# Float64 weights converted in place, with four load buffers and whole pieces per slot, in an attention and mixer kernel

## The chip, the cores and the metric

The kernel runs on one core of one Trainium2 chip. A core has TensorE (PE) for matrix products, VectorE (DVE), ScalarE (ACT) and GpSimd (POOL) for elementwise work, and SyncE (SP), which here only issues transfers. Each takes its own instructions in the order in which the program hands them over. The metric is the device time of the whole kernel in microseconds (us), the median of several runs.

## The reference

Thresholded attention over 8 batches and 8 heads of 576 tokens with 64 columns, then a mixer of two small networks over 512 columns:

```python
scores = scale * np.matmul(q, k.transpose(0, 1, 3, 2))
thresh = np.max(scores, axis=-1, keepdims=True) - tau
scores = np.where(scores >= thresh, scores, -1000000000.0)
attn = np.exp(scores - np.max(scores, axis=-1, keepdims=True))
attn = attn / (np.sum(attn, axis=-1, keepdims=True) + 1e-09)
x = heads side by side of np.matmul(attn, v)          # (8, 576, 512)
h = np.maximum(x.transpose(0, 2, 1) @ w_tok1, 0.0) @ w_tok2
u = x + h.transpose(0, 2, 1)
out = u + np.maximum(u @ w_ch1, 0.0) @ w_ch2
```

The four weight matrices (576x256, 256x576, 512x1536, 1536x512) are scaled by a numpy float64 number when they are made, and so arrive as float64. [...] the kernel makes the float32 values itself, from the two 32-bit halves of each number.

## The kernel before

**Units.** The main loop runs over 144 units (b, w, t), 18 for each of the 8 batches. A unit u covers one block of 128 query rows of two heads. In the order of the code it does the following:

- `scores(u)`: PE makes the scores (L286), DVE takes their maximum (L291, two instructions), POOL turns the maxima into a bias (L292).
- `norm(u - 1)`: DVE takes the reciprocal of the row sums (L310, L311), POOL scales the weights e with it (L314, two instructions).
- The turn of unit u - 2. In batch 0 PE transposes e in three groups (L337), and DVE, or now and then ACT, copies each to eT (L339). In later batches `turn_blocks` transposes on DVE into T (L348), and SP moves the blocks with 16 transfers (L358) whenever a group is complete.
- `weigh(u)`: ACT makes e from the scores, with two Prelu (L301) and two Exp (L304).
- `values`, when due: PE multiplies eT by the values (pv, L388 and L393), ACT copies the result to xT (L398).
- In later batches, mixer steps from the queue `todo`, in up to three places of a unit, by `fill`. `push` fills the queue once a batch has all its values, for batch 0 in unit 20. Its steps are `turn_x` (L412, copied by L413), `tok1` (L422, relu L423), `tok2` (L429, added to xT by DVE at L433), `ch1` (L451, relu L452) and `ch2` (L467).
- `load_qk`, `load_v` and, in some units, `prep`, which transposes q and k of a coming pair on DVE (L268).

A score buffer comes free only when `weigh` has read it, and the two buffers of the mixer's products when ACT or DVE has read them.

**Weights.** The matrices are cut into 31 pieces: two of w1 with 512 columns and one of 64 rows by 256, four of w2 with 288 columns, then 12 of wc1 and 12 of wc2 with 512. `load_piece` brings a piece from HBM into one of three parts of a scratch tile (the tile later serves as xT); SP issues it (L196). `f64_to_f32` converts it with six instructions: on ACT a Copy (L159) of the low words, written over them, and a Square (L160) of the high words into the one buffer h2; on DVE a shift (L161), a sign operation (L164) and a mask (L167), which reads h2; on POOL an add (L168) of the low part, which writes the weight. Between shift and add the value lies in one of two buffers a. Both functions are Python generators: they issue a part and then yield, so that a piece takes three steps.

- Step 1: Copy, Square, shift. Step 2: sign. Step 3: mask, add, and the load of the piece three further on.
- `weight(n)` takes n steps. It stands in two places of a unit: ahead of `weigh(u)`, and after the values. In batch 0 each place takes one step, later four and three.
- `need(i)` takes steps until piece i is converted; the mixer's steps call it ahead of their first use of a weight.

`tc.manual_schedule()` keeps the instructions of every engine in the order in which this code issues them.

Of the kernel before, what the change touches and what calls it, by code (L numbers as in the profile page):

```python
# [9 lines left out]
F32 = mybir.dt.float32  # L10
U32 = mybir.dt.uint32
I32 = mybir.dt.int32
I64 = mybir.dt.int64
AF = mybir.ActivationFunctionType
ALU = mybir.AluOpType
# [6 lines left out]
def kernel(  # L22
# [26 lines left out]
    nc = tc.nc  # L49
# [81 lines left out]

    WMAX = 512
    scratch = work.tile([P, NP * 2 * S], U32, tag="xT", name="scratch")
    NRAW = 3
    raw_at = [scratch[:, 2 * WMAX * i : 2 * WMAX * (i + 1)] for i in range(NRAW)]
    a_at = [scratch[:, 2 * WMAX * NRAW + WMAX * i : 2 * WMAX * NRAW + WMAX * (i + 1)] for i in range(2)]
    sq_at = scratch[:, 2 * WMAX * NRAW + 2 * WMAX : 2 * WMAX * NRAW + 3 * WMAX].bitcast(F32)
    turn_of = [0]

    def like(x, dst):  # L140
        if len(dst.shape) == 2:
            return x
        return x.rearrange("p (a b) -> p a b", a=dst.shape[1])

    def f64_to_f32(dst, raw, rows, n):

        lo, hi = raw[:, :, 0], raw[:, :, 1]
        a = a_at[turn_of[0] % 2][0:rows, 0:n]
        h2 = sq_at[0:rows, 0:n]
        turn_of[0] += 1
        af = a.bitcast(F32)
        nc.scalar.activation(out=lo.bitcast(I32), in_=lo, func=AF.Copy, scale=2.0**-29)  # L159
        nc.scalar.activation(out=h2, in_=hi.bitcast(F32), func=AF.Square)  # L160
        yield nc.vector.tensor_scalar(  # L161
            out=a, in0=hi, scalar1=3, scalar2=0x3FFFFFFF, op0=ALU.logical_shift_left, op1=ALU.bitwise_and
        )
        yield nc.vector.scalar_tensor_tensor(  # L164
            out=a, in0=hi, scalar=0xC0000000, in1=a, op0=ALU.bitwise_and, op1=ALU.bitwise_or
        )
        nc.vector.scalar_tensor_tensor(out=af, in0=h2, scalar=2.0**-30, in1=af, op0=ALU.is_ge, op1=ALU.mult)  # L167
        nc.gpsimd.tensor_tensor(  # L168
            out=dst.bitcast(I32), in0=like(a.bitcast(I32), dst), in1=like(lo.bitcast(I32), dst), op=ALU.add
        )  # L170

    pieces = [
        (w1[:, 2 * i : 2 * i + 2, :], moe_w_tok1[2 * P * i : 2 * P * i + 2 * P, :].rearrange("(t p) x -> p t x", p=P))
        for i in range(NI // 2)
    ]
# [9 lines left out]
    raws = {}  # L185

    def load_piece(i):
        dst, src = pieces[i]
        rows = dst.shape[0]
        n = 1  # L190
        for d in dst.shape[1:]:
            n *= d
        wide = src.dtype == I64
        raw = raw_at[i % NRAW][0:rows, 0 : n * (2 if wide else 1)]
        raw = raw.bitcast(src.dtype)
        nc.sync.dma_start(out=like(raw, dst), in_=src)  # L196
        raws[i] = raw, rows, n

    def weight_ops():
        for i, (dst, src) in enumerate(pieces):  # L200
            raw, rows, n = raws.pop(i)
            if src.dtype == I64:
                for _ in f64_to_f32(dst, raw.bitcast(U32).rearrange("p (n w) -> p n w", w=2), rows, n):
                    yield
            else:
                yield
                yield
                nc.gpsimd.tensor_copy(out=dst, in_=like(raw, dst))
            if i + NRAW < len(pieces):
                load_piece(i + NRAW)  # L210
            yield

    wops = weight_ops()
    steps_done = 0

    def weight(n):

        nonlocal steps_done
        for _ in range(n):
            if next(wops, wops) is wops:  # L220
                return
            steps_done += 1

    def need(i):

        weight(3 * i + 3 - steps_done)

    load_piece(0)
    load_qk(1, (nc.sync, nc.sync))
# [30 lines left out]
    def in_blocks(b):  # L260
        return b > 0
# [10 lines left out]
    def scores(u):  # L272
        b, p0, t = units[u]
        sc = [
            (ps_3rd if b == 0 and (2 * u + h) % 3 == 2 else ps_sc).tile([P, 2, MAIN], F32, tag="sc", name=f"sc{h}_{u}") for h in range(2)
        ]
        if t == SHARED:
            parts = [(b * NP + p0 + i, slice(MAIN, S), slice(64 * i, 64 * i + 64)) for i in range(2)]
        else:
            i, c = divmod(t - (t > SHARED), NI)  # L280
            parts = [(b * NP + p0 + i, slice(P * c, P * c + P), slice(0, P))]
        order = [(f, part, h) for f in range(2) for part in parts for h in range(2)]
        for f, (n, cols, rows), h in order if b else sorted(order, key=lambda o: o[2]):
            r = slice(D * h, D * h + D)
            qT, kT = heads[n]
            nc.tensor.matmul(sc[h][rows, f, 0:HS], lhsT=qT[r, cols], rhs=kT[r, HS * f : HS * f + HS], start=True, stop=True)  # L286
        mx = small.tile([P, 2], F32, tag="mx", name=f"mx_{u}")
        bias = small.tile([P, 2], F32, tag="bias", name=f"bias_{u}")
        for h in range(2):
            c = slice(h, h + 1)  # L290
            nc.vector.tensor_reduce(out=mx[:, c], in_=sc[h][:, :, 0:HS], axis=AX.XY, op=ALU.max)  # L291
            nc.gpsimd.tensor_scalar(out=bias[:, c], in0=mx[:, c], scalar1=toff, scalar2=-SCALE, op0=ALU.add, op1=ALU.mult)  # L292
        st[u] = sc, bias
# [13 lines left out]
    def norm(u):  # L307
        e, rs = st[u]
        rr = small.tile([P, 2], F32, tag="rr", name=f"rr_{u}")
        nc.vector.tensor_scalar(out=rr, in0=rs, scalar1=1e-9, scalar2=None, op0=ALU.add)  # L310
        nc.vector.reciprocal(out=rr, in_=rr)  # L311
        for h in range(2):
            eh = e[:, S * h : S * h + S]
            nc.gpsimd.tensor_scalar(out=eh, in0=eh, scalar1=rr[:, h : h + 1], scalar2=1.0, op0=ALU.mult, op1=ALU.mult)  # L314
        st[u] = e

    def group_of(u):

        b, p0, t = units[u]
        if t == SHARED:  # L320
            return (b, p0, "s"), 0, 1
        i, c = divmod(t - (t > SHARED), NI)
        return (b, p0 + i, c // 2), c % 2, 2
# [38 lines left out]
    def split_middle(n):  # L362

        lv, vl = vals[n], vlast[n % VL]
        for h in range(2):
            r = slice(D * h, D * h + D)
            nc.gpsimd.tensor_copy(out=vl[r, r], in_=lv[r, NI, :])
        vals[n] = lv, vl
# [142 lines left out]
    b_now = 0  # L511
    LAG = 2
    for u in range(len(units) + LAG + 4):
        on = u < len(units)
        if u == UB:
            late.close()
            ps_mm = ctx.enter_context(tc.tile_pool(name="ps_mm", bufs=2, space=bass.MemoryType.PSUM))
        if on:
            b_now, p0, t = units[u]
            n = b_now * NP + p0  # L520
        w = u - LAG
        back = 0 <= w < len(units)
        if on:
            scores(u)
        if 0 < u <= len(units):
            norm(u - 1)
        if back:
            key, place, many = group_of(w)
            if in_blocks(key[0]):
                turn_blocks(w)  # L530
            else:
                for i in range(3):
                    turn(w, i)
            if place == many - 1:
                b, p, c = key
                if c == 0 and p % 2 == 0:
                    split_middle(b * NP + p)
                if c == "s":
                    split_middle(b * NP + p + 1)
                when = u + (2 if in_blocks(b) else 1)  # L540
                due += [(when, b, p + i, c) for i in range(2 if c == "s" else 1)]
        if b_now:
            fill(0.4)
        weight(4 if b_now else 1)
        if on:
            weigh(u)
        if b_now:
            fill(0.3)
        while due and due[0][0] <= u:
            _, b, p, c = due.popleft()  # L550
            values(b, p, c)
            if p == NP - 1 and c == 1:
                push(b)
        if b_now:
            fill(0.3)
        weight(3 if b_now else 1)
        if on:
            m = n + 2 + t // 4
            if t < 8 and m < len(pairs):
                load_qk(m, (nc.scalar if b_now else nc.sync,) * 2, t % 4)  # L560
                if t % 4 == 3:
                    load_v(m)
            if t == 2:
                prep(n + 1)
            if t == 7 and n + 2 < len(pairs):
                prep(n + 2)
    weight(10000)
    quota = 1e9
    fill(1.0)
# [28 lines left out]
```

## Time and profile before

| what | value |
|---|---|
| median of 3 runs | 1424.96 us (1424.34 to 1425.93) |
| the profiled execution: its time, its span | 1424.03 us, 1421.9 us |
| PE busy, share of the span | 1346.7 us, 95% |
| DVE, ACT, POOL busy | 584.1, 589.8, 345.4 us |
| mean granted PE clock | 0.984 |
| Copy L159, Square L160, median of 31 | 0.676, 0.659 us |
| shift L161, sign L164, mask L167, median of 31 | 0.421, 0.823, 0.692 us |
| add L168 with 512 columns, median | 1.367 us |
| first Copy, last mask, last add start at | 8.6, 200.0, 201.1 us |
| weight loads, issue to landing | 2.8 to 6.8 us, median 3.7 |

How to read it: "busy" is the time in which an engine executes. Waits are listed as "engine, instruction <- engine and instruction that released it: total, times, longest". A timeline line gives start, duration, engine, line, operation, output <- input, shapes, count and, in brackets, the idle time ahead of it and its cause. Timeline durations of DVE and ACT contain the ends of pipelines, and follow each other with a small overlap.

### The profile page before, as it was taken

How to read it: one execution, taken by the hardware profiler on the slowest of the kernel's cores; microseconds unless marked ns; L12 is line 12 of the kernel's file. 1: busy time of each engine (PE TensorE's matmuls, PEld its weight loads, DVE VectorE, ACT ScalarE, POOL GpSimd, SP SyncE). 2: the span in 40 equal slices, each digit the busy share in tenths (PEclk: the TensorE clock that was granted, in tenths of full speed). 3: DMA queues.
4: the chain of work that ended last, by engine and by line, in shares of the span. 5: the costliest groups of instructions: out<-in, count | busy, mean ns of one | idle time of the engine just before them, and what ended most of it. 6: DMA issues, size and time to landing. Idle time of an engine off the chain costs nothing.

```text
span 1421.9 us, 19495 instructions
## 1 busy us (share of the span) xinstructions
PE 1346.7 (95%) x6866; PEld 832.4 (59%) x6866; DVE 584.1 (41%) x1009; ACT 589.8 (41%) x1328; POOL 345.4 (24%) x681
## 2 busy tenths in 40 slices
PE   6777689988999999999999999999999999999998
PEld 4443455645656566565656566566657466566675
DVE  5888654344344443434433444334333443201000
ACT  5776353443545444353434444353334344220110
POOL 4565332222222222222212222222121222100000
PEclk9998899989999999999999999999999999999999
DMA  6344544443444434443343534443433433300000
GB/s 130 90 117 131 152 125 103 92 116 84 102 120 111 108 84 106 104 98 80 92 101 77 121 80 111 104 98 69 103 87 83 111 91 78 82 15 15 8 8 23
DMA packets 257376, 128.34 MB, mean 90 GB/s; under 512 B 208064, under 2 KB 221376, under 8 KB 257280
## 3 DMA queue, kind: packets, MB, share of 16 engines
q1 hardware_dynamic: 131632, 111.46, 29.9%
q10 hardware_dynamic: 125648, 15.64, 6.9%
q8 instruction: 55, 0.90, 0.3%
q14 instruction: 41, 0.34, 0.1%
HBM read 43.25 MB, written 9.44 MB: 37 GB/s over the span
## 4 chain that ended last, share of the span: by engine, by line
PE 81%; DVE 8%; SPq 5%; DMA 3%; ACT 3%; issue 1%; POOL 0%; DVEq 0%; ACTq 0%
PE c L467 26%; PE c L451 24%; PE sc L286 10%; PE pv L393 7%; SPq L358 5%; PE t L422 3%; PE t L429 3%; DVE mx L291 3%; PE pv L388 2%; DVE T L348 2%; PE tx L412 2%; PE c L463 1%; DMA eT<-T 1%; DMA scratch<-in_moe_w_ch_dram 1%; ACT e L301 1%
## 5 line engine op out<-in xcount | busy, mean ns | idle before, releaser
L451 PE MATMUL c<-xT,wc 128*128 128x256 f32 (+1 forms) x1920 | 406.2, 363 | 1.9 <-DVE xT L433 0.8
L291 DVE TENSOR_REDUCE mx<-sc 128x1 f32<-128x576 f32 x288 | 204.6, 751 | 489.5 <-PE sc L286 489.4
L467 PE MATMUL c<-wc,g 128*128 128x512 f32 x864 | 389.5, 597 | 0.0
L451 PEld LDWEIGHTS c<-xT,wc 128*128 128x128 f32 x1920 | 331.7, 190 | 75.9 <-issue 29.9
L292 POOL TENSOR_SCALAR bias<-mx,toff 128x1 f32<-128x1 f32 x288 | 76.7, 267 | 807.8 <-DVE mx L291 754.1
L301 ACT ACTIVATE e<-sc,bias 128x576 f32<-128x576 f32 x288 | 199.2, 741 | 169.7 <-POOL bias L292 148.8
L467 PEld LDWEIGHTS c<-wc,g 128*128 128x128 f32 x864 | 157.6, 190 | 177.3 <-issue 175.9
L452 ACT ACTIVATE g<-c 128x256 f32<-128x256 f32 (+1 forms) x240 | 87.3, 364 | 386.0 <-PE c L451 366.5
L304 ACT ACTIVATE e<-e,ntau 128x576 f32<-128x576 f32 x288 | 220.8, 774 | 0.0
L314 POOL TENSOR_SCALAR e<-e,rr 128x576 f32<-128x576 f32 x288 | 213.4, 753 | 17.3 <-DVE rr L311 4.1
L286 PE MATMUL sc<-kT,qT 64*128 64x288 f32 (+1 forms) x1280 | 196.7, 441 | 20.0 <-ACT e L301 10.9
L348 DVE STREAM_TRANSPOSE T<-e 128x1152 f32<-128x1152 f32 x126 | 172.5, 1369 | 16.5 <-DMA eT<-T 10.8
L286 PEld LDWEIGHTS sc<-kT,qT 64*128 64x128 f32 (+1 forms) x1280 | 107.1, 181 | 102.1 <-issue 50.1
L393 PE MATMUL pv<-eT,lv 128*64 128x256 f32 x1024 | 124.0, 385 | 0.0
L472 DVE COPY o<-c 128x512 f32<-128x512 f32 x36 | 24.6, 684 | 192.7 <-PE c L467 192.7
L393 PEld LDWEIGHTS pv<-eT,lv 128*64 128x64 f32 x1024 | 75.7, 140 | 38.0 <-issue 2.6
L429 PE MATMUL t<-w,a 128*128 128x288 f32 x256 | 78.8, 437 | 17.8 <-DVE xT L433 15.8
L422 PE MATMUL t<-x,w 128*128 128x512 f32 (+1 forms) x160 | 76.0, 613 | 0.0
L429 PEld LDWEIGHTS t<-w,a 128*128 128x128 f32 x256 | 46.7, 197 | 42.6 <-DVE xT L433 20.8
L398 ACT COPY xT<-pv 128x256 f32<-128x256 f32 x64 | 23.9, 373 | 107.4 <-PE pv L393 107.3
L433 DVE TENSOR_TENSOR xT<-xT,t 128x288 f32<-128x288 f32 x64 | 27.9, 442 | 96.5 <-PE t L429 96.4
L304 ACT ACTIVATION_READ_ACCUMULATOR e<-e,ntau 128x1 f32 x288 | 57.4, 199 | 0.0
(43 smaller groups left out, 600.4 us busy)
## 6 DMA issues: line engine op xcount, KB each, us to landing
eT<-T SPq DMA_DIRECT2D x896, 72.0 KB, 2.0
scratch<-in_moe_w_ch_dram SPq DMA_DIRECT2D x24, 512.0 KB, 3.8
lv<-in_v_dram SPq DMA_DIRECT2D x32, 288.0 KB, 3.3
out_dram<-o SPq DMA_DIRECT2D x36, 256.0 KB, 2.2
eT<-T SPq DMA_DIRECT2D x224, 36.0 KB, 1.9
lk<-in_k_dram ACTq DMA_DIRECT2D x108, 72.0 KB, 2.7
lq<-in_q_dram ACTq DMA_DIRECT2D x104, 72.0 KB, 2.1
lq<-in_q_dram SPq DMA_DIRECT2D x24, 72.0 KB, 3.3
```

What stands on the lines that cost most here:

```text
L286: nc.tensor.matmul(sc[h][rows, f, 0:HS], lhsT=qT[r, cols], rhs=kT[r, HS * f : HS * f + HS], start=True, stop=True)
L291: nc.vector.tensor_reduce(out=mx[:, c], in_=sc[h][:, :, 0:HS], axis=AX.XY, op=ALU.max)
L301: nc.scalar.activation(out=eh, in_=sc[h][:, :, 0:HS], func=AF.Prelu, bias=bias[:, h : h + 1], scale=SCALE, alpha=STEEP)
L304: nc.scalar.activation(out=eh, in_=eh, func=AF.Exp, bias=ntau, accum_out=rs[:, h : h + 1])
L314: nc.gpsimd.tensor_scalar(out=eh, in0=eh, scalar1=rr[:, h : h + 1], scalar2=1.0, op0=ALU.mult, op1=ALU.mult)
L348: nc.vector.transpose(out=T.rearrange("p (a c n x) -> p c a n x", a=4, c=NK, n=n)[:, :, :, place, :], in_=e.rearrange("p (c a x) -> p c a ...
L393: nc.tensor.matmul(to[r], lhsT=lv[:, j, :], rhs=eT[:, j], start=False, stop=(c == NI - 1), skip_group_check=True)
L422: nc.tensor.matmul(ps, lhsT=w1[0:M, t, P * m : P * m + P], rhs=s["x"][0:M, t, :], start=(t == 0), stop=(t == NT - 1))
L429: nc.tensor.matmul(ps, lhsT=s["a"][:, m, P * c : P * c + P], rhs=w2[:, m, HS * f : HS * f + HS], start=(m == 0), stop=(m == NTK - 1))
L451: nc.tensor.matmul(ps, lhsT=wc1[:, j, c, :], rhs=uT[:, c, GR * i : GR * i + n], start=(c == 0), stop=(c == NCC - 1))
L452: nc.scalar.activation(out=s["g"][:, j, 0:n], in_=ps, func=AF.Relu)
L467: nc.tensor.matmul(flat, lhsT=s["g"][:, j, P * t : P * t + P], rhs=wc2[:, j, :], start=False, stop=(j == NJ - 1), skip_group_check=True)
```

## The change

The two buffers a are dropped: shift, sign and mask write into the weight's own tile, and the add works on it in place. There are four load buffers instead of three. The conversion is no longer cut into steps: `weight(n)` converts n whole pieces. After piece i, from piece 1 on, the load of piece i + 3 is asked for, which now uses the buffer of piece i - 1. In batch 0 a piece is converted at the end of a unit, in three units out of four. In later batches one is converted ahead of the turn of unit u - 2, and one at the end.

```diff
-    NRAW = 3
+    NRAW = 4
     raw_at = [scratch[:, 2 * WMAX * i : 2 * WMAX * (i + 1)] for i in range(NRAW)]
-    a_at = [scratch[...] for i in range(2)]
-    sq_at = scratch[:, 2 * WMAX * NRAW + 2 * WMAX : 2 * WMAX * NRAW + 3 * WMAX].bitcast(F32)
-    turn_of = [0]
+    sq_at = scratch[:, 2 * WMAX * NRAW : 2 * WMAX * NRAW + WMAX].bitcast(F32)
...
-        lo, hi = raw[:, :, 0], raw[:, :, 1]
-        a = a_at[turn_of[0] % 2][0:rows, 0:n]
-        h2 = sq_at[0:rows, 0:n]
-        turn_of[0] += 1
-        af = a.bitcast(F32)
+        lo, hi = like(raw[:, :, 0], dst), like(raw[:, :, 1], dst)
+        h2 = like(sq_at[0:rows, 0:n], dst)
+        bits = dst.bitcast(U32)
         nc.scalar.activation(out=lo.bitcast(I32), in_=lo, func=AF.Copy, scale=2.0**-29)
         nc.scalar.activation(out=h2, in_=hi.bitcast(F32), func=AF.Square)
-        yield nc.vector.tensor_scalar(out=a, in0=hi, ...)
-        yield nc.vector.scalar_tensor_tensor(out=a, in0=hi, scalar=0xC0000000, in1=a, ...)
-        nc.vector.scalar_tensor_tensor(out=af, in0=h2, scalar=2.0**-30, in1=af, op0=ALU.is_ge, op1=ALU.mult)
-        nc.gpsimd.tensor_tensor(out=dst.bitcast(I32), in0=like(a.bitcast(I32), dst), in1=like(lo.bitcast(I32), dst), op=ALU.add)
+        nc.vector.tensor_scalar(out=bits, in0=hi, ...)
+        nc.vector.scalar_tensor_tensor(out=bits, in0=hi, scalar=0xC0000000, in1=bits, ...)
+        nc.vector.scalar_tensor_tensor(out=dst, in0=h2, scalar=2.0**-30, in1=dst, op0=ALU.is_ge, op1=ALU.mult)
+        nc.gpsimd.tensor_tensor(out=dst.bitcast(I32), in0=dst.bitcast(I32), in1=lo.bitcast(I32), op=ALU.add)
...
-    def weight_ops():
-        for i, (dst, src) in enumerate(pieces):
+    def weight(n):
+        nonlocal done
+        for i in range(done, min(done + n, len(pieces))):
+            dst, src = pieces[i]
...
-            if i + NRAW < len(pieces):
-                load_piece(i + NRAW)
-            yield
+            if 0 < i < len(pieces) - NRAW + 1:
+                load_piece(i + NRAW - 1)
+            done = i + 1
...
         if 0 < u <= len(units):
             norm(u - 1)
+        if b_now:
+            weight(1)
         if back:
...
         if b_now:
             fill(0.4)
-        weight(4 if b_now else 1)
         if on:
             weigh(u)
...
         if b_now:
             fill(0.3)
-        weight(3 if b_now else 1)
+        weight(1 if b_now or u % 4 < 3 else 0)
```

More of the change, by code (lines that the diff above doesn't have):

```diff
@@ L133 @@
     scratch = work.tile([P, NP * 2 * S], U32, tag="xT", name="scratch")
-    NRAW = 3
+    NRAW = 4
     raw_at = [scratch[:, 2 * WMAX * i : 2 * WMAX * (i + 1)] for i in range(NRAW)]
-    a_at = [scratch[:, 2 * WMAX * NRAW + WMAX * i : 2 * WMAX * NRAW + WMAX * (i + 1)] for i in range(2)]
-    sq_at = scratch[:, 2 * WMAX * NRAW + 2 * WMAX : 2 * WMAX * NRAW + 3 * WMAX].bitcast(F32)
-    turn_of = [0]
+    sq_at = scratch[:, 2 * WMAX * NRAW : 2 * WMAX * NRAW + WMAX].bitcast(F32)
     def like(x, dst):
@@ L145, in f64_to_f32 @@
     def f64_to_f32(dst, raw, rows, n):
-        lo, hi = raw[:, :, 0], raw[:, :, 1]
-        a = a_at[turn_of[0] % 2][0:rows, 0:n]
-        h2 = sq_at[0:rows, 0:n]
-        turn_of[0] += 1
-        af = a.bitcast(F32)
+        lo, hi = like(raw[:, :, 0], dst), like(raw[:, :, 1], dst)
+        h2 = like(sq_at[0:rows, 0:n], dst)
+        bits = dst.bitcast(U32)
         nc.scalar.activation(out=lo.bitcast(I32), in_=lo, func=AF.Copy, scale=2.0**-29)
         nc.scalar.activation(out=h2, in_=hi.bitcast(F32), func=AF.Square)
-        yield nc.vector.tensor_scalar(
-            out=a, in0=hi, scalar1=3, scalar2=0x3FFFFFFF, op0=ALU.logical_shift_left, op1=ALU.bitwise_and
-        )
-        yield nc.vector.scalar_tensor_tensor(
-            out=a, in0=hi, scalar=0xC0000000, in1=a, op0=ALU.bitwise_and, op1=ALU.bitwise_or
-        )
[L167 to L170, printed above, removed]
+        nc.vector.tensor_scalar(
+            out=bits, in0=hi, scalar1=3, scalar2=0x3FFFFFFF, op0=ALU.logical_shift_left, op1=ALU.bitwise_and
+        )
+        nc.vector.scalar_tensor_tensor(
+            out=bits, in0=hi, scalar=0xC0000000, in1=bits, op0=ALU.bitwise_and, op1=ALU.bitwise_or
+        )
+        nc.vector.scalar_tensor_tensor(out=dst, in0=h2, scalar=2.0**-30, in1=dst, op0=ALU.is_ge, op1=ALU.mult)
+        nc.gpsimd.tensor_tensor(out=dst.bitcast(I32), in0=dst.bitcast(I32), in1=lo.bitcast(I32), op=ALU.add)
     pieces = [
@@ L197, in load_piece @@
         raws[i] = raw, rows, n
-    def weight_ops():
-        for i, (dst, src) in enumerate(pieces):
-            raw, rows, n = raws.pop(i)
+    done = 0
+    def weight(n):
+        nonlocal done
+        for i in range(done, min(done + n, len(pieces))):
+            dst, src = pieces[i]
+            raw, rows, m = raws.pop(i)
             if src.dtype == I64:
-                for _ in f64_to_f32(dst, raw.bitcast(U32).rearrange("p (n w) -> p n w", w=2), rows, n):
-                    yield
-            else:
-                yield
-                yield
+                f64_to_f32(dst, raw.bitcast(U32).rearrange("p (n w) -> p n w", w=2), rows, m)
+            else:
                 nc.gpsimd.tensor_copy(out=dst, in_=like(raw, dst))
-            if i + NRAW < len(pieces):
-                load_piece(i + NRAW)
[L211 to L222, printed above, removed]
+            if 0 < i < len(pieces) - NRAW + 1:
+                load_piece(i + NRAW - 1)
+            done = i + 1
     def need(i):
-        weight(3 * i + 3 - steps_done)
+        weight(i + 1 - done)
     load_piece(0)
@@ L566 @@
                 prep(n + 2)
-    weight(10000)
+    weight(len(pieces))
     quota = 1e9
```

## The prediction

> **What bounds the kernel now.** I read the page's slices first, then windows, then waits, then the timeline of one unit. Names: unit u is one pass of the main loop; mx(u) is its first L291; "a piece" is the six-instruction conversion Copy L159 and Square L160 (ACT), shift L161, sign L164, mask L167 (DVE), add L168 (POOL).
>
> ```profile
> PE   6777689988999999999999999999999999999998
> PEclk9998899989999999999999999999999999999999
> ```
>
> A slice is 35.5 us. From slice 6 on TensorE is full but for slices 8 and 9, so whatever is won or lost before about 206 us moves the end by as much. All 31 pieces run there (last add at 201.1).
>
> ```profile
> 11.00:101.00 90.00, 71.47 (x512) 45.51 (x509) 72.93 (x155) 68.94 (x150) 52.56 (x90) 1.00 0.45 107
> 101.00:119.00 18.00, 11.26 (x52) 6.55 (x54) 16.20 (x28) 11.48 (x24) 10.62 (x13) 0.73 0.48 135
> 119.00:174.00 55.00, 39.14 (x165) 22.38 (x162) 38.42 (x59) 26.96 (x52) 21.47 (x28) 0.84 0.50 135
> 174.00:206.00 32.00, 27.70 (x161) 20.55 (x161) 20.72 (x32) 18.22 (x42) 14.03 (x20) 0.95 0.49 140
> ```
>
> Columns: stretch, us, busy PE, PEld, DVE, ACT, POOL, clock, DMA share, GB/s. The first stretch is batch 0 (units 0 to 17): PE, DVE and ACT all near 80%, a relay between them. The rest is units 18 to 26: PE idles 6.7 + 15.9 + 4.3 = 26.9 us at a lowered clock. Waits of 101 to 206 us:
>
> ```profile
> ACT scratch L160 <- DVE scratch L167: 16.7, 6, 4.5
> ACT scratch L159 <- DMA scratch<-in_moe_w_ch_dram: 14.6, 4, 7.1
> PE t L429 <- DVE xT L433: 11.1, 2, 8.0
> DVE scratch L161 <- DMA scratch<-in_moe_w_ch_dram: 9.5, 3, 4.3
> DVE scratch L167 <- ACT scratch L160: 7.8, 2, 4.3
> ```
>
> So there pieces wait for loads, and for each other's one square buffer; scores and residual adds stand behind them. The last line matters most: the mask needs the square from ACT, and in 31 pieces it waited for it only twice, never before 119 us, because the generator puts mask and square at least one slot apart. Unit 10, DVE then ACT:
>
> ```profile
> 60.34 1.42 DVE L291 TENSOR_REDUCE mx<-sc 128x1 f32<-128x576 f32 x2 [2.04 <-PE sc L286]
> ...
> 64.30 1.42 DVE L291 TENSOR_REDUCE mx<-sc 128x1 f32<-128x576 f32 x2
> ```
> ```profile
> 64.22 0.19 ACT L304 ACTIVATION_READ_ACCUMULATOR e<-e,ntau 128x1 f32 x1
> 64.31 0.68 ACT L159 ACTIVATE scratch<-scratch 128x512 int32<-128x512 uint32 x1
> 64.89 0.64 ACT L160 ACTIVATE scratch<-scratch 128x512 f32<-128x512 f32 x1
> ```
>
> mx(10) to mx(11) is 3.96 us, yet the Square issued in that unit ends at 65.5, 5.2 us after mx(10): it stands behind both Exp of the unit.
>
> **The skill.** The Trainium skill, "TensorE: Matmul & The Clock Gate", opening table, gives ScalarE, VectorE and GpSimd strict first-in-first-out queues. The trace agrees: at 106.25 a Square that waited 4.14 us held e(18), and PE's next scores with it. Same page, "What's actually happening": little PE activity in a 3.4 us window halves the clock. Agrees: the first lowered clock follows the 3.38 us idle before 115.44. "SBUF — State Buffer", "Who interferes with whom": a DVE instruction with two SBUF inputs and a GpSimd one exclude each other. Agrees: sign L164 takes 0.69 us alone and 1.66 when it starts inside an L168 (106.59 against 106.30).
>
> **The change part by part.**
>
> *In place, without the two buffers a.* Instruction counts, widths and forms stay: 31 x 6. No row shows a wait for a buffer a (L161 waits only for DMA), and matrices are read first at unit 21. Zero; bounds -0.5 to +0.5 us.
>
> *Four load buffers, load one piece later.* Still 31 loads, and after piece i still the load of i+3; but its buffer is that of piece i-1, whose add is long done. SP's waits on L168 (35.7 us in nine times between 84 and 206) fall away; 16 eT transfers at some 0.63 us each no longer stand behind them. In slot one the load now goes ahead of the 16 (10 us). Only the second load of a unit that issues eT comes after, and lands about 6 + 10 + 4 = 20 us after that mx; it is needed two units on, at about 20. I take the ACT and DVE waits on loads as gone; what is late next is below.
>
> *Whole pieces, batch 0.* Fourteen pieces instead of twelve, each at the end of a unit, behind weigh(u) and the xT copies on ACT. Shift, sign and mask now follow each other on DVE, and mx(u+1) stands behind the mask. New loop: mx(u), bias, two Prelu, two Exp, Copy, Square, mask, mx(u+1): 3.97 us to the last Exp (60.34 to 64.31), 1.22 for Copy and Square, 0.05, 0.65 for the mask: 5.9 us. At 288 columns: 3.97 + 0.85 + 0.4 = 5.2.
> - Units 10, 12, 14, 17 (no value product, 512 columns): 3.96 + 4.28 + 4.66 + 4.25 = 17.15 now, 4 x 5.9 = 23.6 then; for 10 and 14 the bias also stands behind the 1.37 us add of the piece before, 0.6 each: **+7.7**.
> - Units 5 and 8 (288): 8.0 to 10.4: **+2.4**.
> - Units 4, 6, 9, 13, 16: ACT's xT copy ends 5.5, 5.5, 5.0, 5.1, 4.5 after mx; plus 1.2 or 1.9 for squares and mask, 1.4 more for prep in 16: 6.75 + 6.7 + 6.9 + 7.0 + 7.8 = 35.15, against 29.8: **+5.3**.
> - Units 0 to 2: now 13.7 us from mx(0) to mx(3). Then 5.9, 6.75 (bias behind add) and 7.5 (64-row piece, prep): 20.2: **+6.5**.
> - Units 3, 7, 11, 15 have no piece: 0, as PE's pv and scores or eT copies bound them.
>
> Sum +21.9; bounds +14 (if ACT gets ahead somewhere) and +26.
>
> *Slots apart, units 18 to 23.* Two pieces a unit instead of 2.33. The first stands ahead of turn_blocks; its Square is early on ACT, but sign waits for the 1.46 us L314 pair on POOL, so it takes some 3.1 us of DVE (2.0 bare) before T. The second mask waits behind e, ACT's copies and relus. Mx to mx, worked with the durations above:
> - 18: eT copies end at 6.4, pv and its copy 9.2, squares 10.5, mask: 11.2 (now 8.6). 19: 7.7 (9.5).
> - 20: xT copy 5.3, five tx steps to 10.4, squares, mask: 12.3 (15.0). 21: second tok1 product and relu 8.8, squares, mask: 10.7 (8.4).
> - 22: adds of t behind mx, piece and T, done 8.9, then the piece: 10.6 (17.8). 23: four t, pv 11.3, one c and relu 13.7, squares, mask: 15.6 (13.6).
>
> Sum 68.1 against 72.9: **-4.8**; bounds -15 (PE's work at full clock fits in less) and +3 (loads late, or PE at half clock).
>
> *From unit 24.* Now PE still loses 1.75 + 0.55 + 2.0 idle, some 2 in broken scores (2.79 against 1.2) and 1.7 at half clock: 8. Then PE runs ahead of DVE by two c groups; I leave 2 of loss: **-6**; bounds -8 and -1.
>
> *Clock.* In batch 0 PE now gets about 2.7 us of work in 5.9 us units, with gaps near 3.8 us. Nothing of batch 0 before 101 us shows a lowered clock. A slow window costs up to 2.4 us where pv stands in it, nothing elsewhere: **+3**; bounds 0 and +10.
>
> Sum: 21.9 - 4.8 - 6 + 3 = +14. The profiled execution took 1424.03 us (span 1421.9), 0.9 under the median of 1424.96: predicted **1438**, from 1438.0 on its scale and 1439 on the median's, rounded down. About 0.2%, 2.8 us, is what a measurement here can tell from no change.
>
> **Rivals.**
> 1. *The waits on loads decide: faster.* Place: units 18 to 26. PE waits there behind Square, load and add sum to 3.38 + 0.51 + 4.69 + 8.03 + 3.02 + 1.75 + 2.0 = 23.4 us. If all go, and batch 0 pays only DVE time of two more pieces (2 x 1.8), 1424 - 23.4 + 3.6 = 1404; with half my loss in batch 0, 1412. It decides once a batch-0 piece delays less than (23.4 - 2.8) / 14 = 1.5 us, provided all waits go. For it: the 8.03 us wait, whose origin is a load behind 16 transfers. Against: the second mask makes a new wait in the same units. Chance 0.12.
> 2. *PE goes cold: much slower.* Ten value products of 2.4 us in batch 0 doubled in half of the cases, +12, and the token steps in 20 to 23 with them: 1450. For it: clock 0.73 where PE was 63% busy. Against: clock 1.00 in batch 0. Chance 0.18.
> 3. *Cancellation, or a mask that waits for nothing new:* ACT ahead of DVE wherever a piece stands. Then the loss of batch 0 is near its lower bound and gains near theirs: 1424 + 14 - 10 - 6 = 1422. For it: only 7.8 us of mask waits today. Against: Square stands behind Exp of the same unit in the changed order. Chance 0.08.
> 4. *As worked out,* 1430 to 1446: 0.62.
>
> **Numbers.** Slower takes 4, 2 and a little of 3: 0.80. No change 0.07, faster 0.13. The range 1424 to 1452 leaves out most of 1 and the tail of 2.
>
> **What would show it.** Right: the mask L163 (as it is numbered then) waits for Square L156, 1 to 2 us at most pieces and over 20 us in all; mx(18) at about 122 us instead of 100.7; SP's waits on the add and ACT's on loads near zero; PE full from about unit 24. Wrong: mx(18) before 112 us, or mask waits under 8 us (step on batch 0); units 18 to 23 under 60 us or over 75 (step on the slots); a clock of 0.8 in batch 0 (rival 2); ACT waits on loads that remain (step on loads).

## The result, and the profile after

The changed kernel takes 1443.18 us (median of 4 runs, 1442.82 to 1445.15) against 1424.86 us: 1.013 of the kernel before, 95% interval 1.0113 to 1.0148. It is 18.3 us slower. The profiled execution took 1445.15 us (span 1443.3), 21.1 us more than that of before.

In the page's slices of the changed kernel (36.1 us each, counted from 0 as in the prediction), PE is lower in slices 0, 2 and 3, and its clock in slices 2, 3 and 9; the others differ little from before:

```profile
PE   5766789988999999999999999999999999999998
PEclk9987899997999999999999999999999999999999
```

Four stretches of it: units 0 to 13, units 14 to 16, unit 17 to the middle of 23, and from there into unit 26 (columns: stretch, us, busy PE, PEld, DVE, ACT, POOL, clock, DMA share, GB/s):

```profile
11.00:101.00 90.00, 64.20 (x388) 39.40 (x384) 57.85 (x124) 55.38 (x119) 39.51 (x70) 0.92 0.42 100
101.00:123.00 22.00, 15.78 (x114) 9.84 (x114) 13.05 (x28) 12.39 (x27) 9.69 (x17) 0.77 0.35 83
123.00:190.00 67.00, 44.55 (x183) 25.01 (x183) 48.49 (x84) 39.46 (x76) 37.35 (x43) 0.79 0.45 130
190.00:225.00 35.00, 33.92 (x204) 24.85 (x204) 23.20 (x37) 20.19 (x45) 17.98 (x20) 0.95 0.44 117
```

From 11 to 101 us DVE is busy 57.9 us where it was 72.9, and ACT 55.4 instead of 68.9: the kernel before finished all 18 units of batch 0 in that time, the changed one finishes 14. For what it waits, this list tells (in the changed code the mask is L163, Square L156, Copy L155, the product t L414 and the scores' maximum L276):

```profile
DVE wc L163 <- ACT scratch L156: 29.8, 13, 4.7
DVE w L163 <- ACT scratch L156: 14.5, 7, 3.7
PE t L414 <- DVE xT L418: 9.3, 2, 4.7
ACT scratch L155 <- DMA scratch<-in_moe_w_ch_dram: 6.9, 2, 4.1
ACT scratch L156 <- DVE wc L163: 3.4, 8, 1.3
```

Twenty masks of 31 wait for the Square, 44.3 us in all, against 7.8 us in two before. The other waits that the prediction listed became smaller. Unit 10 again, DVE from its mx to the next, then ACT around its Square:

```profile
73.24 1.41 DVE L276 TENSOR_REDUCE mx<-sc 128x1 f32<-128x576 f32 x2
...
76.95 0.70 DVE L160 SCALAR_TENSOR_TENSOR wc<-scratch,wc 128x512 uint32<-128x512 uint32 x1
78.96 0.69 DVE L163 SCALAR_TENSOR_TENSOR wc<-scratch,wc 128x512 f32<-128x512 f32 x1 [1.31 <-ACT scratch L156]
79.57 0.75 DVE L276 TENSOR_REDUCE mx<-sc 128x1 f32<-128x576 f32 x1
```
```profile
77.65 0.19 ACT L289 ACTIVATION_READ_ACCUMULATOR e<-e,ntau 128x1 f32 x1
77.74 0.64 ACT L155 ACTIVATE scratch<-scratch 128x512 int32<-128x512 uint32 x1
78.28 0.65 ACT L156 ACTIVATE scratch<-scratch 128x512 f32<-128x512 f32 x1
```

The sign is through at 77.65, the Square behind both Exp only at 78.9; mask and mx(11) follow. The spacing is 6.33 us where it was 3.96.

Where the time went, from mx to mx in the two profiled executions:

| stretch | before | after | difference | predicted |
|---|---|---|---|---|
| up to mx(0) | 11.4 | 12.0 | +0.6 | 0 |
| mx(0) to mx(18), batch 0 | 89.3 | 117.1 | +27.7 | +21.9, and +3 for the clock |
| mx(18) to mx(24) | 72.9 | 70.2 | -2.8 | -4.8 |
| mx(24) to mx(26) | 23.6 | 18.7 | -4.9 | -6 |
| the rest of the span | 1224.8 | 1225.4 | +0.7 | 0 |

### The profile page after: what moved, and what is told of

It reads as the page before. It is cut to its first block, busy times and chain, and to the rows that moved or that the text cites. A ratio compares the mean times of both kernels' runs of the same rounds, so it can differ in the third digit from the quotient of the medians.

```text
span 1443.3 us, 19465 instructions
## 1 busy us (share of the span) xinstructions
PE 1356.3 (94%) x6866; PEld 836.4 (58%) x6866; DVE 578.2 (40%) x1009; ACT 588.9 (41%) x1328; POOL 351.2 (24%) x681
## 4 chain that ended last, share of the span: by engine, by line
PE 80%; DVE 7%; ACT 4%; SPq 4%; DMA 2%; issue 1%; POOL 1%; ACTq 0%; DVEq 0%
PE c L452 26%; PE c L436 23%; PE sc L271 10%; PE pv L378 8%; PE t L407 4%; SPq L343 4%; PE t L414 3%; PE pv L373 3%; DVE mx L276 2%; DVE T L333 2%; PE tx L397 1%; ACT e L289 1%; ACT e L286 1%; PE c L448 1%; DMA eT<-T 1%
## 5 line engine op out<-in xcount | busy, mean ns | idle before, releaser
L276 DVE TENSOR_REDUCE mx<-sc 128x1 f32<-128x576 f32 x288 | 204.4, 751 | 488.9 <-PE sc L271 488.9
L286 ACT ACTIVATE e<-sc,bias 128x576 f32<-128x576 f32 x288 | 198.7, 739 | 199.7 <-POOL bias L277 178.7
L299 POOL TENSOR_SCALAR e<-e,rr 128x576 f32<-128x576 f32 x288 | 220.5, 778 | 15.9 <-DVE rr L296 4.0
L271 PE MATMUL sc<-kT,qT 64*128 64x288 f32 (+1 forms) x1280 | 197.3, 444 | 18.7 <-DVE kT L253 10.1
L378 PE MATMUL pv<-eT,lv 128*64 128x256 f32 x1024 | 131.2, 401 | 0.0
L378 PEld LDWEIGHTS pv<-eT,lv 128*64 128x64 f32 x1024 | 78.7, 145 | 41.6 <-issue 8.7
L414 PE MATMUL t<-w,a 128*128 128x288 f32 x256 | 78.4, 436 | 15.9 <-DVE xT L418 14.0
L414 PEld LDWEIGHTS t<-w,a 128*128 128x128 f32 x256 | 47.0, 198 | 40.4 <-DVE xT L418 19.0
L373 PE MATMUL pv<-eT,vl 128*64 128x256 f32 x256 | 44.6, 428 | 13.5 <-DVE eT L324 6.9
```

The costliest lines, as they stand in the source:

```text
L286: nc.scalar.activation(out=eh, in_=sc[h][:, :, 0:HS], func=AF.Prelu, bias=bias[:, h : h + 1], scale=SCALE, alpha=STEEP)
L373: nc.tensor.matmul(to[r], lhsT=vl[:, r], rhs=eT[:, NI], start=True, stop=False, skip_group_check=True)
L378: nc.tensor.matmul(to[r], lhsT=lv[:, j, :], rhs=eT[:, j], start=False, stop=(c == NI - 1), skip_group_check=True)
L414: nc.tensor.matmul(ps, lhsT=s["a"][:, m, P * c : P * c + P], rhs=w2[:, m, HS * f : HS * f + HS], start=(m == 0), stop=(m == NTK - 1))
```

## The experiments

Theory A is that of the prediction: a mask issued in the same slot as its Square waits on ACT, and mx waits behind the mask. Theory B: a whole piece is too much DVE work between two scores, whatever it waits for. Theory C: loads, buffers or the conversion in place are at fault. The groups ran on different chips, on which the kernel before took 1424.9, 1420.9, 1420.7 and 1421.3 us; so kernels of different groups are compared by their ratio to the kernel before.

### The mask without the Square

```diff
-nc.vector.scalar_tensor_tensor(out=dst, in0=h2, scalar=2.0**-30, in1=dst, ...)
+nc.vector.scalar_tensor_tensor(out=dst, in0=hi.bitcast(F32), scalar=2.0**-30, in1=dst, ...)
```

> The changed kernel, but the mask compares the high word itself instead of its square (negative weights are zeroed, so the output is not the reference's); Copy and Square still run on ACT, at the same places. Theory A (the mask stands behind the Square, and mx behind the mask): no mask waits for ACT any more; mx(18) comes at 104 to 108 us instead of 129, and the time falls from 1443 to 1410 to 1420, under the kernel before. Theory B (a whole piece in one slot is too much DVE work between scores, whatever it waits for): mx(18) stays above 118, time 1433 or more. Theory C (loads, four buffers or conversion in place are at fault): 1443, as nothing of them is touched.

Measured: 1413.59 us, 0.9949 (0.9928 to 0.997). No mask waits for ACT, mx(18) comes at 105.8. Removing one input, with all instructions in place, takes back the whole loss and more. The clock goes with it: it is 1.00 from 31 to 109 us. Theory C falls as the cause of the loss, and B as its main cause. This kernel leaves out the negative weights, which become zero; the next one, with the full arithmetic, gains as much. Mx(0) to mx(18) takes 96.3 us, 7 more than before: there are two more pieces, and they are grouped. How the 7 us divide is not shown.

### The Square earlier

```diff
         if b_now:
+            squares(2)
             weight(1)
...
+        if not b_now and u % 4 < 3:
+            squares(1)
         if on:
             weigh(u)
```

`squares(n)` issues Copy and Square of the next n pieces. The Square has a second buffer here, which the changed kernel lacks, and in later batches both pairs of a unit stand in the first slot.

> The changed kernel with its full arithmetic, but Copy and Square of the pieces of a unit are issued ahead of weigh(u) (in later batches both pairs in the first slot, with a second buffer for the square); shift, sign, mask and add stay where they are. Theory A: ACT does the pair while it waits for the bias, about 2 us in most units, so mask waits fall from 44 us to under 12 and the time to 1413 to 1423. Theory B: 1435 or more. Theory C: 1443.

Measured: 1415.0 us, 0.9956 (0.9941 to 0.9971), with the full arithmetic. There is no mask wait left. Unit 10 in this kernel (shift L165, sign L168, mask L171, maximum L295), DVE, then ACT:

```profile
63.87 0.69 DVE L168 SCALAR_TENSOR_TENSOR wc<-scratch,wc 128x512 uint32<-128x512 uint32 x1
64.66 0.69 DVE L171 SCALAR_TENSOR_TENSOR wc<-scratch,wc 128x512 f32<-128x512 f32 x1
65.27 1.42 DVE L295 TENSOR_REDUCE mx<-sc 128x1 f32<-128x576 f32 x2
```
```profile
59.19 0.68 ACT L150 ACTIVATE scratch<-scratch 128x512 int32<-128x512 uint32 x1
59.77 0.67 ACT L151 ACTIVATE scratch<-scratch 128x512 f32<-128x512 f32 x1
61.30 1.40 ACT L305 ACTIVATE e<-sc,bias 128x576 f32<-128x576 f32 x2 [0.86 <-POOL bias L296]
```

ACT makes the pair while it would have waited for the bias, and still waits 0.86 us for it. The kernel beats both the one before and the changed one. So the place of the Square is enough to remove the loss, given that second buffer. In the changed kernel the Square's own waits for the one buffer are 3.4 us in all.

### New loads alone, and conversion in place alone

```diff
 # both, in the kernel before: shift, sign and mask write into dst
 # the first of the two also:
-    NRAW = 3
+    NRAW = 4
-            if i + NRAW < len(pieces):
-                load_piece(i + NRAW)
+            if 0 < i < len(pieces) - NRAW + 1:
+                load_piece(i + NRAW - 1)
```

> The kernel before with its three steps and its slots, but with conversion in place, four buffers and the load one piece later: one half of the change alone. Theory A: mask waits stay below 10 us, the SP waits on the add go, ACT waits on loads fall from 14.6 us to under 8, and the time is 1410 to 1421. Theory B: the same. Theory C: slower than 1428.

> The kernel before with conversion in place alone: three buffers, three steps, old slots. Theories A and B: 1424 to 1426, no row waits for a buffer a today. Theory C with conversion in place at fault (a new wait, or a slower instruction): 1430 or more.

Measured: 1423.28 us, 1.001 (0.9995 to 1.0025), and 1420.86 us, 1.0002 (0.9986 to 1.0017). In place costs nothing, as predicted. The new loads alone gain nothing: here the expectation of 1410 to 1421 was missed. The waits of that kernel from 101 to 215 us (Copy L156, shift L158), and what SP issues ahead of the longest:

```profile
ACT scratch L156 <- DMA scratch<-in_moe_w_ch_dram: 11.2, 3, 6.5
DVE wc L158 <- DMA scratch<-in_moe_w_ch_dram: 8.5, 3, 3.5
```
```profile
138.32 10.06 SPq L355 DMA_DIRECT2D eT<-T  x16
148.49 1.02 SPq L193 DMA_DIRECT2D scratch<-in_moe_w_ch_dram  x2
```

The longest of these waits ends at 152.48, when the first load behind the 16 transfers of eT lands. The kernel before has the same order there (16 transfers from 136.82, loads from 146.98, a wait of 7.1 us that ends at 151.13), so the fourth buffer did not help there. SP's waits for an add remain too, 37.8 us in ten; in these SP reached a load before its buffer was free. Mx(18) to mx(24) takes 72.7 us, as before (72.9).

### What shortens units 18 to 26

Three variants of the kernel with the Square earlier:

```diff
 # old loads
-    NRAW = 4
+    NRAW = 3
...
-            if 0 < i < len(pieces) - NRAW + 1:
-                load_piece(i + NRAW - 1)
+            if i + NRAW < len(pieces):
+                load_piece(i + NRAW)
 # first slot behind the turn
         if b_now:
-            squares(2)
-            weight(1)
...
         if b_now:
             fill(0.4)
+            squares(2)
+            weight(1)
 # twelve pieces in batch 0, at squares and at weight
-u % 4 < 3
+u % 3 < 2
```

> The kernel with the squares ahead of weigh (1415.0), but with three load buffers and the old rule for loads (after piece i, the load of i + 3 into the buffer that piece i has just left). Theory A1 (the slots and the smaller number of pieces per unit shorten units 18 to 26, the loads hardly): 1414 to 1418. Theory A2 (the fourth buffer and the later load do it, once pieces stand apart): the SP waits on the add grow by 20 us or more, and 1420 to 1426.

> The kernel with the squares ahead of weigh, but in later batches the first slot stands where the kernel before has it, behind the turn and the first mixer steps, so that its load comes behind the 16 eT transfers. Theory A1 with the place of the first slot as its cause: ACT and DVE waits on loads rise from 7 us to 15 or more, 1420 to 1425. Theory A1 with two pieces instead of 2.33 as its cause: 1413 to 1417; slightly faster even, since T and the residual adds come ahead of the piece on DVE.

> The kernel with the squares ahead of weigh, but with a piece in two of three units of batch 0: 12 as in the kernel before, so that 19 are left for units 18 to 27. Mx(18) should come 2 to 4 us earlier than 106. If units 18 to 26 gain because fewer pieces are left, they lose it again: 1416 to 1420. If they gain by the two slots alone, 1411 to 1414.

Measured: 1421.11 us, 1.0006 (0.9992 to 1.0019); 1417.28 us, 0.9973 (0.9962 to 0.9984); 1417.34 us, 0.9976 (0.9966 to 0.9987). Against 0.9956 each one is worse in its middle, but only the old loads stand clear of that kernel's interval. With pieces apart, then, the four buffers and the later load are worth something, which they are not with steps. How much is not settled. In the profiled executions mx(0) to mx(18) takes 96.4 us with old loads against 94.9, and mx(18) to mx(24) 65.3 against 64.1; the two whole executions are 2.1 us apart (1417.5 and 1415.4), the medians 6.1. With the first slot behind the turn, the waits of ACT and DVE on weight loads are 17.0 us, against 10.0 with the Square earlier. That is what the theory of the place said, but the time stays under its 1420 to 1425. With twelve pieces in batch 0 mx(18) comes 94.2 us after mx(0), not the 2 to 4 us earlier that was expected. Units 9 and 11 take 7.7 and 7.5 us there, against 5.9 and 5.9 with fourteen pieces, and the clock is 0.51 from 54 to 61 us and 0.57 from 71 to 75. Mx(18) to mx(24) takes 65.6 us. The place of the first slot and the number of pieces in batch 0 matter less than these runs can tell from the spread.

### The clock in batch 0

The changed kernel once more, on the chip of the last group, and with more work for PE where it waits in batch 0:

```diff
-                nc.tensor.transpose(out=ps[:, c, :], in_=e[:, k0 : k0 + P], identity=ident)
+                for _ in range(3 if third < 2 else 1):            # first try
+                for _ in range(3 if third < 2 and u >= 4 else 1): # second
+                    nc.tensor.transpose(out=ps[:, c, :], in_=e[:, k0 : k0 + P], identity=ident)
```

> The changed kernel, with PE's transposes of the first two thirds of e in batch 0 made three times over (same result, 1.8 us more work a unit, mostly where PE waited 1.5 to 4 us for DVE's eT copies). Theory A with the clock as its second part: the slow windows of batch 0 (five of them between 50 and 129 us, clock near 0.6) mostly go, the spacings 6 to 7, 9 to 10, 12 to 13 and 15 to 16 fall from about 8.3 to 6 to 7 us, mx(18) comes at 120 to 125 instead of 129, and the time is 1435 to 1440. Rival: the added PE work is in the way and the slow clock cost nothing: 1443 to 1452.

> The changed kernel as it is, on the chip of the other kernels of this group, so that they can be set against it directly: 1.011 to 1.015 of the kernel before.

> The changed kernel with the first two thirds of PE's transposes of e in batch 0 made three times over, but only from unit 4 on, when PE has warmed up. If the slow clock in the units with a value product is what batch 0 cost beyond the mask waits (8 us of 28), mx(0) to mx(18) falls from 117 to 109 to 112 us and the time to 1.006 to 1.010 of the kernel before. If the slow clock cost nothing, 1.012 or more.

Measured: first try 1438.93 us, 1.0127 (1.0107 to 1.0148), not to be told from the changed kernel. Three stretches of 3.4 us at half clock were left, from 32.3, 49.4 and 107.4 us, and units 4, 6 and 15, in which they fall, take 8.4, 8.2 and 7.5 us. Why they were left is not shown. The changed kernel again: 1441.29 us, 1.0148 (1.0121 to 1.0175). From unit 4 on: 1434.93 us, 1.0096 (1.0077 to 1.0114), 6.4 us faster with more work. From 80 us to the end of batch 0, the changed kernel again:

```profile
80.00:101.00 21.00, 14.20 (x99) 8.79 (x97) 12.75 (x28) 11.60 (x24) 9.66 (x16) 0.90 0.30 71
101.00:129.00 28.00, 18.97 (x121) 11.45 (x119) 17.81 (x37) 17.35 (x38) 12.11 (x20) 0.69 0.33 81
```

and the same two stretches with the added transposes from unit 4 on, where batch 0 ends at 120 us:

```profile
80.00:101.00 21.00, 17.54 (x146) 13.08 (x143) 14.53 (x30) 14.11 (x30) 9.80 (x17) 1.00 0.43 97
101.00:129.00 28.00, 20.66 (x172) 14.33 (x174) 19.33 (x39) 16.21 (x35) 14.59 (x22) 0.94 0.32 92
```

Mask waits hardly change (42.8 and 40.7 us), the clock does, and mx(0) to mx(18) falls from 116.4 to 110.5 us. Three spacings with a value product, units 6, 11 and 15, hold it: 25.2 us together in the first, 18.3 in the second. Units 7 and 9 take 0.7 and 0.5 us more, the others hardly move.

### Whole pieces alone

```diff
-                for _ in f64_to_f32(...):
-                    yield
+                yield
+                yield
+                for _ in f64_to_f32(...):
+                    pass
```

> The kernel before with its buffers, loads and slots, but steps 1 and 2 of a piece are empty and the six instructions stand together in step 3: whole pieces alone. Theory A: the half of them that fall ahead of weigh wait little, the half behind weigh wait for the Square as in the changed kernel; in batch 0 six of twelve, at 1.5 to 2.5 us each, with more waits in units 18 to 26: mask waits 20 to 40 us, 1.005 to 1.012 of the kernel before. Theory C (loads, buffers or place at fault): 0.998 to 1.002.

Measured: 1427.64 us, 1.0052 (1.003 to 1.0074). Slower, in the stated range; mask waits are 17.2 us in 11, under the 20 to 40 expected. Batch 0 grew more than these waits say: mx(0) to mx(18) is 104.7 us, 15.4 more than before, with 6.6 us of mask waits up to 116 us; the clock is low there too (0.88 from 80 to 101 us). Units 18 to 25 give 6.9 us back. So waits for the Square are not the only cost of whole pieces in the old slots; what the rest is divided into was not tried.

### Pieces beside value products

```diff
-u % 4 < 3
+u in (0, 1, 2, 4, 6, 7, 9, 10, 11, 12, 13, 14, 15, 16)
```

> The kernel with the squares ahead of weigh, 14 pieces in batch 0 as there, but in other units: 5, 8 and 17 give theirs to 7, 11 and 15, where a value product on PE stands between eT copies and the next scores, and DVE has some 2 us. If DVE's own work is what is left of the cost of pieces in batch 0, mx(0) to mx(18) falls from 94.9 us to 91 to 93 and the ratio to the kernel before from 0.9956 to 0.992 to 0.995. If not, 0.9956 or more.

Measured: 1415.64 us, 0.9956 (0.9939 to 0.9973), the same as with the Square earlier. The expected 0.992 to 0.995 was missed. Mx(0) to mx(18) is 93.6 us, 1.3 less, but the end does not come earlier by an amount that can be seen. These runs show no gain from this choice of units.

## Why the prediction was right, and where its steps were off

It said 1438 us and slower, with 1424 to 1452; measured were 1443. The terms that were off by more than 1 us all fell short in the same sense, so the result does not rest on errors that cancel.

- **The mask behind the Square: right, and shown.** The loop of 5.9 us was worked out from one unit of the kernel before. Units 5, 8, 10, 12, 14 and 17 were to take 35.2 us; they take 34.7. "Mask waits over 20 us" are 44.3. Without the dependency the loss is gone.
- **Startup: a little high.** Units 0 to 2 take 19.2 us, predicted 20.2.
- **The clock: the term that was mis-sized.** It stood at +3. Units 6 and 9 take 3.0 us more than the sum had, and units 11 and 15, which it booked at 0 since they have no piece, 5.3 more than before: 8.3 together. That is most of the way from mx(18) at 122, as forecast, to 129. Their windows show the reason:

```profile
50.00:54.00 4.00, 4.00 (x22) 2.11 (x20) 0.74 (x2) 1.40 (x5) 0.35 (x2) 0.59 0.95 199
66.00:71.00 5.00, 3.94 (x22) 2.11 (x22) 2.88 (x7) 2.88 (x6) 2.04 (x4) 0.66 0.54 134
80.00:88.00 8.00, 6.23 (x29) 3.30 (x29) 3.49 (x8) 3.25 (x7) 2.92 (x5) 0.57 0.50 121
108.00:116.00 8.00, 6.60 (x33) 3.77 (x34) 2.16 (x6) 3.25 (x7) 2.96 (x7) 0.58 0.49 121
```

These are the four units in which a value product and the scores behind it run at half clock. The experiment with more work for PE took 6.4 us back. Rival 2 had the mechanism, at +12; the truth lies between. The term leaned on gaps near 3.8 us, which do not even fit its own loop: 5.9 us with 2.7 us of work leave 3.2. From 46 to 125 us the gaps are 3.35 us once and otherwise at most 2.4, and half clock came all the same. The evidence was misread too: the first lowered clock of the kernel before is not the one after the 3.38 us wait at 115.44. A finer window of the kernel before has it already here, after a wait of 2.17 us:

```profile
103.00:106.00 3.00, 3.00 (x15) 1.74 (x17) 2.33 (x5) 0.00 (x0) 1.03 (x2) 0.53 0.54 175
```

Nor was batch 0 at full clock from its start, as the 1.00 of its window was read. The trace has no clock record before 30.8 us, and the view counts that as 1.00. But the score products of 64x288 (L286) average 719 ns from 12 to 30 us and 429 from 32 to 101.

- **Units 18 to 23: right in sign, -2.8 instead of -4.8.** Unit by unit 11.9, 7.5, 12.4, 10.2, 11.5 and 16.6 us, against 11.2, 7.7, 12.3, 10.7, 10.6 and 15.6. The 18.1 us of mask waits from 130 us on, up to 4.7 at a time, are the new wait that the prediction named.
- **Loads: half right.** ACT's waits on loads fell from 14.6 to 6.9 us, not to none; the one of 4.1 us at 180.95 is for the load behind the 16 transfers that was called just in time. That the buffers by themselves would take the waits away was wrong: with the old steps they stay (11.2 and 8.5 us). SP's waits did not go either, they changed sides: between 84 and 215 us it waits 39.4 us for a Square and 15.7 us for an add.
- **From unit 24: right**, -4.9 against -6.
- **Conversion in place: zero, as said.** Rival 1, in which the loads decide, is out. A gain exists, though: once the Square is out of the way, the new slots with the new loads are faster than the kernel before by 6 us. Neither does it alone: the new slots with old loads stand at 1.0006, the old steps with new loads at 1.001.

## What to carry to other kernels

Ahead of joining split work into one block, look where its parts run: if one part stands on another engine behind that unit's long chain, the block gets the latency of that chain, and every instruction behind it too. Issue the part on the other engine one slot earlier, where that engine waits anyway. And where a relay of engines bounds a stage, ask what share of the time PE will still be busy: a slower relay can also lower its clock, and then units that the change does not touch get longer.

## What the runs showed of the hardware that was not expected

More work on PE made a kernel faster: 1.0096 instead of 1.0148 of the kernel before, by transposes done three times over, because the granted clock rose. And half clock came without a long gap of PE, none over 2.4 us just ahead of three of the four slow stretches of the changed kernel. In the 3.4 us ahead of the four (from 49.9, 66.9, 80.6 and 104.5 us) PE was busy 1.1 to 1.5 us; ahead of the first of the kernel before (from 102.4), 1.6. In the kernel whose mask reads the high word PE was busy 53.6 of the 78 us from 31 to 109, and no slow stretch came. These figures point to how busy PE was over a few us, and not to one long gap; that this is the rule, and where its limit lies, is not shown.

The clock also goes with the spread between runs of one program. In the twelve runs with old loads, those with a mean clock of 0.987 or 0.988 took 1417.1 to 1418.6 us, those with 0.983 to 0.985 took 1420.9 to 1424.3 us; so a difference of a few us between two kernels should be looked at together with their clocks. In other groups the tie is looser.
